# One-core gated spectral and token-MLP kernel: renumbered odd wavenumbers, pairs of 64-row inverse products, filter rows in two slabs, a 16-partition special line

## Chip, cores and metric

The kernel runs on one core of a Trainium2 chip. The metric is the device time of one execution in microseconds (us); several executions are made and the median is compared. The profile is of one execution more.

## What is computed

```python
x = A_x                                            # 1 x 2048 x 512, bf16
g = sigmoid((x * gate_w).sum(-1, keepdims=True))   # one gate value per row
a = irfft2(rfft2(x.float()) * (w_r + 1j * w_i))    # filter: 2048 x 257 complex
h = layernorm(x)                                   # over d
u = gelu(einsum("bsd,sf->bdf", h, w1) + b1)        # f = 1792
y = einsum("bdf,fs->bds", u, w2) + b2
out = g * a + (1 - g) * y.transpose(0, 2, 1)
```

s (2048 rows) is the direction of the token MLP and of the complex transform; d (512 columns) is that of the real transform. All data are bf16, sums of products f32.

## The kernel before

**Staging.** Row s = 512 q + 4 a + r is kept on partition a. The MLP has two large products, each 14 pieces ft of 128 hidden units by 16 row blocks j, each a full-array 128x512 product: m1 (L716) with W1 (`wa`, `wb`), and m2 (L1065) with W2, whose pieces come into the buffers that W1 has left. The gelu (L732, ScalarE) turns m1's sums into `gl`, the operand of m2; L1071 (ScalarE) or L1078 (VectorE) takes m2's sums out of PSUM.

The spectral branch lies among these products. Forward transform along s: products with the table `ta` (L565 to L568), eviction to `xp`, radix-4 additions on VectorE (L596 to L612); the wavenumbers are split in even ones (lt=0, two halves of 64 partitions) and odd ones (lt=1). Special columns of d are corrected by small VectorE operations (`sp0`, `sp1`, L621 to L639). Forward transform along d (L664), evicted by L671 into `X`; `tb2` (L680 to L688) makes sums and differences of mirrored rows into `B`. The filter: `W` holds w_r and w_i in the order of the wavenumbers, `wt` rows that have to be mirrored over the partitions by a product with a flipped identity (`flip`, L768, evicted by L772); `wprep` (L789, L790), and the complex multiplication on VectorE (`bfly` L831/832, `mul` L839, `comb` L844/845, `ob` L851 to L853). Column 0 and 256 have their own small path (`c0a` L800/801, `c0b` L820 to L825, `c0c` L858/859), and wavenumber 1024 (the "special line") is worked on one partition (`nyq`, L810 to L815), goes with eight lines more by DMA into `s9`, through one product (`linem`, L871, evicted L873), and back into `B` by a DMA. `omg` (L752 to L754) makes (1-g)/2-like factors out of the gate.

Inverse along s: radix-4 on VectorE, then products with the table `ti`: even residues (L929 to L934), odd residues of the odd wavenumbers as full-array 128x256 products (`i1`, L925), odd residues of the even wavenumbers as 64-row products in two halves of the array (`i1s`, L897). ScalarE evicts them (L900, L940, L945), VectorE joins the halves (`eo2` L905, `zf` L953 to L959, `fq` L965/966). Inverse along d: `i3` (L1008 to L1012), evicted with the gate as factor by L1016, joined by L1025 and L1042 to L1049, added to the MLP part (L1078, L1084) and stored.

**What sets the order.** Every step is a task with an engine, an author's duration, the tasks it depends on, a priority and PSUM banks that it takes and frees (`add`, L151). `order` (L173) runs through time by these durations, lets each engine take the ready task of lowest priority number, and so writes one list; the instructions are emitted in this order and each engine runs its own in order. Banks: "acc" four, "fa" two, "fb" two. A matmul task for m1 or m2 is one product, an inverse task one group of products.

**Loads.** All loads are issued by SyncE (SP) through `dma` (L312) in one queue; each waits in the built program for one of eight semaphores in turn, that is for the load eight before it. Order: x and tables, W1's first columns (`wa`, `wb`), `b2h` (8-byte packets), the filter `ld_W(0)` of w_r, W1's last columns (`wb`), `ld_W(1)` of w_i, then W2 into `wa` and `wb`, with the inverse tables `ti` (in the buffer "rot") and `tg` between. `ld_W` makes 16 DMAs for a component, among them four "turned" ones, in which the rows are read in descending order within slabs:

```python
for e in range(4):
    dma(W[:, 1, e, 1, 0:257], v[:, 3 - e, 3, :].rearrange("(o i) l -> o i l", o=4)[:, ::-1])
for o in range(4):
    dma(W[32 * o:32 * o + 32, 1, :, 0, 0:257], v[96 - 32 * o:128 - 32 * o, :, 1, :])
```

Of the kernel before, what the change touches and what calls it, by code (L numbers as in the profile page):

```python
# [16 lines left out]
P = 128  # L17
# [13 lines left out]
def ti_at(r):  # L31
    return (0, 1024, 512, 1920)[r], (512, 896)[r % 2]


def make_tables():

    p = np.arange(P)
    r4 = np.arange(4)
# [6 lines left out]
    ti = np.zeros((P, 3072))  # L45
    for r in range(4):
# [6 lines left out]
        th = ang(s, 1 + 4 * (p ^ 96), S)  # L53
# [7 lines left out]
        if r % 2:  # L61
            sg = np.where(p < 64, 1.0, -1.0)[:, None]
            th = ang(k, s, S)
            v = v.reshape(P, 7, P)
            v[:, 0] = np.cos(th)
            v[:, 1] = sg * np.cos(th)
            v[:, 2] = -np.sin(th)
            v[:, 3] = -sg * np.sin(th)
            v[0, 2:4] = alt * (0.5 ** 0.5 if r == 1 else -(0.5 ** 0.5))
            th = ang(1 + 4 * (p ^ 96), s, S)  # L70
            v[:, 4] = -np.sin(th)
            v[:, 5] = np.cos(th)
            v[:, 6] = np.sin(th)
            ti[:, o:o + w] = v.reshape(P, w)
        else:
            s5 = np.append(s, 512)
            for lt, kk in enumerate((k, 1 + 4 * (p ^ 96))):
                th = ang(kk, s5, S)
                c, n = np.cos(th), -np.sin(th)
                if lt == 0:  # L80
                    n[0, 0:P] = 0.0 if r == 0 else -alt
                u = v[:, 256 * lt:256 * lt + 256]
                u[:, 0:P], u[:, P:] = c[:, 0:P], n[:, 0:P]
                if r == 0 and lt:
                    u[:, P] = -n[:, P]
                elif r == 0:
                    ti[:, 2816:2879], ti[:, 2943:3007] = n[:, 2:P:2], n[:, 1:P:2]
                    u[:, 0:65], u[:, 66:130] = c[:, 0:129:2], c[:, 1:P:2]
                    u[0, 66:130], ti[0, 2879:2943] = 0.0, 1.0
# [49 lines left out]
class Plan:  # L139
# [33 lines left out]
    def order(self):  # L173
# [17 lines left out]
        while events:  # L191
# [19 lines left out]
            while progress:  # L211
                progress = False
                for eng, ts in pending.items():
# [57 lines left out]
def kernel(  # L271
# [42 lines left out]
    def alloc_first():  # L314
# [15 lines left out]
        t["wn"] = sb([1, 2, WL], BF16, "wn")  # L330
# [3 lines left out]
        t["sp"] = sb([P, 4, 2, 4], F32, "sp")  # L334
# [3 lines left out]
        t["cm"] = sb([P, 4, 4, 2], F32, "cm")  # L338
# [95 lines left out]

    def ld_W(comp):
# [24 lines left out]
    def ld_ti():  # L460
        t["ti"] = sb([P, 3072], BF16, "rot")
# [158 lines left out]
    def sp0():  # L620
        V.tensor_copy(t["sp"][:], t["X"][:, 0, :, :, :, 0])  # L621
    dk = [("D", r) for r in range(4)]
    add("DVE", tiny(1), sp0, reads=dk, writes=["sp"], prio=0)

    def sp1():
        sp, sd, fx = t["sp"], t["sd"], t["fx"]
# [7 lines left out]
        V.tensor_scalar_mul(sd[:, 0, 0, 1], sd[:, 1, 1, 1], c)  # L634
        V.tensor_scalar_mul(sd[:, 1, 0, 1], sd[:, 0, 1, 1], -c)
        V.tensor_add(fx[:, 1, 0], sp[:, 0, 1], sd[:, 0, 0, 1])
        V.tensor_sub(fx[:, 3, 0], sp[:, 0, 1], sd[:, 0, 0, 1])
        V.tensor_sub(fx[:, 1, 1], sd[:, 1, 0, 1], sp[:, 2, 1])
        V.tensor_add(fx[:, 3, 1], sd[:, 1, 0, 1], sp[:, 2, 1])  # L639
    add("DVE", tiny(12), sp1, reads=["sp"], writes=["fx"], prio=0)  # L640

    for lt in (0, 1):
# [3 lines left out]
               dk + ([] if lt else ["sp"]), [("Z", lt, 0), ("Z", lt, 1)], pr, False)  # L646
# [9 lines left out]
    for lt in (0, 1):  # L656
        for e in (0, 2, 1, 3):
# [16 lines left out]

            if e >= 2:
                def tb2(lt=lt, e0=e - 2):
# [13 lines left out]
                add("DVE", tt(1024) + 2 * tt(508) + tiny(6) * (e > 2), tb2, reads=[("R", lt, i, c) for i in (e - 2, e) for c in range(2)],  # L690
                    writes=[("B", lt, i) for i in es_], prio=2.5)


# [57 lines left out]
    def omg():  # L751
        V.tensor_scalar(t["omg"][:], t["g"][:], -0.5, 0.5, op0=Alu.mult, op1=Alu.add)  # L752
        V.tensor_scalar(t["g"][:], t["g"][:], 0.5, 0.5, op0=Alu.mult, op1=Alu.add)
        V.tensor_mul(t["ombb2"][:], t["omg"][:], t["b2h"][:].rearrange("p q r -> p (q r)"))  # L754
    add("DVE", 0.4, omg, reads=["b2h"], writes=["g", "omg"], prio=0)


    add("SP", 0.2, ld_ti, writes=["ti"], prio=39, nbytes=754176, after=[pl.last_w["pa", r, dq] for r in range(4) for dq in range(4)])
# [35 lines left out]
    for lt in range(2):  # L794
# [3 lines left out]
        def c0a(lt=lt):  # L798
            b, c0 = t["B"][:, lt], t["c0"][:, lt]
            V.tensor_copy(c0[:, :, 0, :], b[:, :, 0:2, 0])  # L800
            V.tensor_copy(c0[:, :, 1, :], b[:, :, 3:1:-1, 0])
        add("DVE", 0.2, c0a, reads=bk, writes=[("c0", lt)], prio=0)
        if lt == 0:
            def nyq():
                pz = sb([1, 1280], F32, "X")
                na = pz[:, 0:1024].rearrange("p (i v l) -> p i v l", i=2, v=2)
                nn = t["nn"] = pz[:, 1024:1280].bitcast(BF16).rearrange("p (v l) -> p v l", v=2)
                wn, v = t["wn"], t["B"][0:1, 0, 0, 2:4, :]
                for i in range(2):
                    V.tensor_mul(na[:, i], v, wn[:, i, None, 0:L].to_broadcast([1, 2, L]))  # L810
                V.tensor_sub(nn[:, 0], na[:, 0, 1], na[:, 1, 0])
                V.tensor_add(nn[:, 1], na[:, 1, 1], na[:, 0, 0])
                V.tensor_mul(pz[:, 0:2], t["c0"][0:1, 0, 0, 1, :], wn[:, 0, 0:257:256])
                V.tensor_add(nn[:, 0, 0:1], pz[:, 0:1], pz[:, 1:2])
                V.tensor_sub(nn[:, 1, 0:1], pz[:, 0:1], pz[:, 1:2])  # L815
            add("DVE", 3 * d1(512) + 0.35, nyq, reads=[("B", i, e) for i in range(2) for e in range(4)] + [("W", 0), ("W", 1), ("c0", 0)] + pbk, writes=["nn"], prio=0.5)

        def c0b(lt=lt):
            c0, cm, ce, pm = t["c0"][:, lt], t["cm"], t["ce"][:, lt], t["wpm"]
            V.tensor_mul(cm[:, 0], c0[:, :, 0], pm[:, 0, lt])  # L820
            V.tensor_mul(cm[:, 1], c0[:, :, 1], pm[:, 1, lt])
            V.tensor_mul(cm[:, 2], c0[:, :, 0], pm[:, 1, lt])
            V.tensor_mul(cm[:, 3], c0[:, :, 1], pm[:, 0, lt])
            V.tensor_sub(ce[:, :, 0], cm[:, 0], cm[:, 1])
            V.tensor_add(ce[:, :, 1], cm[:, 2], cm[:, 3])  # L825
        add("DVE", tiny(6), c0b, reads=[("c0", lt), "wpm"], writes=[("ce", lt)], prio=0.3)
# [35 lines left out]
        if lt == 0:  # L862
            def lines():
                t["s8"] = sb([P, D], BF16, "s8")
                dma(t["s9"][0:8], t["B"][0:1, 0].rearrange("p e (c v) l -> p (e c) (v l)", c=2))
                dma(t["s9"][8:9], t["nn"].rearrange("p v l -> p (v l)"))
# [19 lines left out]
    i1t = {}  # L886
    for rs, h in ((0, 0), (0, 1), (1, 0), (1, 1)):
        if rs:
            def i1s(h=h):
                p2 = t["i1s", h] = [ps([P, 2, 2, P], F32, tag, 2) for tag in ("fa", "fb")]  # L890
                for n, r in enumerate((1, 3)):
                    ti = t["ti"][:, ti_at(r)[0]:]
                    for v in range(2):
                        for c in range(2):
                            for m in range(2):
                                k = slice(64 * m, 64 * m + 64)
                                T.matmul(p2[m][:, n, v], lhsT=t["B"][k, 0, r, 2 * c + v, h:L:2], rhs=ti[k, 2 * c * P:2 * c * P + P], start=(c == 0), stop=(c == 1))  # L897
            i1t[h, 1, 0] = i1t[h, 3, 0] = add("PE", MMR, i1s, reads=[("T", 0, 1), "ti"], writes=[("i1s", h)], prio=3, alloc=["fa", "fb"])
            for m in range(2):
                add("ACT", act(512), lambda h=h, m=m: A.copy(t["zo"][:, h, m], t["i1s", h][m][:]), reads=[("i1s", h)] + pbk, writes=[("zo", h, m)],  # L900
                    prio=1.7, free=[("fa", "fb")[m]], after=[lined])

            def eo2(h=h):
                for k, f in enumerate((V.tensor_add, V.tensor_sub)):
                    f(t["zz"][:, 1, h, 0, :, k].rearrange("p v r a -> p r v a"), t["zo"][:, h, 0], t["zo"][:, h, 1])  # L905
            add("DVE", 2 * tt(512), eo2, reads=[("zo", h, m) for m in range(2)], writes=[("zz", h, r, 0) for r in (1, 3)], prio=3.55)
        for r in (rs, rs + 2):
            for lt in range(rs, 2):
                tag = ("fa", "fb")[lt if not rs else r // 2]

                def i1(h=h, r=r, lt=lt, tag=tag):
                    if "zz" not in t:
# [220 lines left out]
```

## Time and profile before

| | |
|---|---|
| median of 3 executions | 126.05 us (125.95 to 126.53) |
| profiled execution | 126.11 us, span 124.3 us, granted TensorE clock 1.000 |
| TensorE (PE) busy | 119.8 us, 96%, 789 products |
| VectorE (DVE) busy | 113.2 us, 91%, 271 instructions |
| ScalarE (ACT) busy | 83.7 us, 67%, 176 instructions |
| DMA | 23.10 MB, mean 186 GB/s |
| m1 (L716), all groups | 27.0 + 17.1 + 9.9 + 6.1 us busy |
| m2 (L1065), two large groups | 24.7 + 24.0 us busy |

The span is the time from the first to the last instruction; the execution's own time is 1.8 us longer. PE's busy time is that of pipelined products; what a product costs in a row of others is read from the distance of the starts (0.216 us for 128x512), not from its duration of 372 to 379 ns. The page's DMA line (busy tenths in 40 slices of 3.1 us) and the rate under it show when the loads run:

```profile
DMA  3999999992459946699999930000000000003751
GB/s 112 316 329 306 397 394 385 376 300 62 112 121 258 289 97 121 157 395 406 420 414 415 422 132 0 0 5 0 3 0 0 5 0 0 0 12 131 287 211 42
```

### The profile page before, as it was taken

The numbers are of one execution on the slowest core, as the hardware profiler recorded it, in microseconds if no ns is written. First come the engines' busy times: TensorE is split into PE (matmuls) and PEld (weight loads), VectorE is DVE, ScalarE is ACT, GpSimd is POOL, SyncE is SP. The second block draws the span as 40 slices with busy tenths as digits, with TensorE's granted clock in tenths as the row PEclk, the third lists the DMA queues.
The fourth block names the chain that finished last, engine by engine and source line by source line (L and its number), as shares of the span: only waits on it lengthen the run. The fifth ranks groups of instructions, "written<-read, shape, count | busy, mean of one in ns | idle before, by whom it ended". The sixth has DMA issues, their size and how long they took to land.

```text
span 124.3 us, 2226 instructions
## 1 busy us (share of the span) xinstructions
PE 119.8 (96%) x789; PEld 67.7 (54%) x789; DVE 113.2 (91%) x271; ACT 83.7 (67%) x176; POOL 0.2 (0%) x4
## 2 busy tenths in 40 slices
PE   7799999999999999999999999999999999999990
PEld 2245555555645466644445555555577576665590
DVE  1789999999999999999999999999969999999951
ACT  3696889699999999999520003742279999993200
POOL 0000000000000000000000000000000000000000
PEclk9999999999999999999999999999999999999999
DMA  3999999992459946699999930000000000003751
GB/s 112 316 329 306 397 394 385 376 300 62 112 121 258 289 97 121 157 395 406 420 414 415 422 132 0 0 5 0 3 0 0 5 0 0 0 12 131 287 211 42
DMA packets 18203, 23.10 MB, mean 186 GB/s; under 512 B 2174, under 2 KB 15888, under 8 KB 18192
## 3 DMA queue, kind: packets, MB, share of 16 engines
q1 hardware_dynamic: 17616, 22.34, 52.9%
q10 hardware_dynamic: 576, 0.62, 1.6%
q8 instruction: 6, 0.10, 0.3%
q14 instruction: 5, 0.04, 0.1%
HBM read 20.84 MB, written 2.10 MB: 185 GB/s over the span
## 4 chain that ended last, share of the span: by engine, by line
PE 93%; DMA 2%; DVE 1%; ACT 0%; issue 0%
PE acc L1065 33%; PE acc L716 31%; PE fb L716 6%; PE fb L1065 6%; PE fa L716 3%; DMA x<-in_A_x_dram 2%; PE fb L664 1%; PE fa L664 1%; PE fa L565 1%; PE fa L566 1%; PE fa L897 1%; PE fb L1012 1%; PE fa L1012 1%; PE fa L568 1%; PE fa L567 1%; PE fb L925 1%
## 5 line engine op out<-in xcount | busy, mean ns | idle before, releaser
L716 PE MATMUL acc<-h,wb 128*128 128x512 bf16 x112 | 27.0, 379 | 0.0
L1065 PE MATMUL acc<-gl,wb 128*128 128x512 bf16 (+1 forms) x98 | 24.7, 372 | 0.0
L1065 PE MATMUL acc<-gl,wa 128*128 128x512 bf16 (+1 forms) x98 | 24.0, 371 | 0.0
L1071 ACT ACTIVATE x<-acc,ombb,omg 128x512 bf16<-128x512 f32 x12 | 9.0, 780 | 19.3 <-PE acc L1065 19.3
L1065 PEld LDWEIGHTS <-wa 128*128 128x128 bf16 x126 | 13.4, 113 | 9.6
L1065 PEld LDWEIGHTS <-wb 128*128 128x128 bf16 x126 | 13.2, 114 | 9.4
L716 PE MATMUL acc<-h,wa 128*128 128x512 bf16 x64 | 17.1, 379 | 0.0
L716 PEld LDWEIGHTS <-wb 128*128 128x128 bf16 x112 | 10.7, 98 | 10.3
L716 PEld LDWEIGHTS <-wa 128*128 128x128 bf16 x112 | 10.3, 98 | 10.9 <-DMA wa<-in_B_w_dram 1.1
L489 DVE BATCH_NORM_STATS2 stats<-x 128x6 f32<-128x512 bf16 x12 | 8.1, 676 | 2.1 <-DMA x<-in_A_x_dram 2.1
L746 ACT ACTIVATE x<-x 128x512 bf16<-128x512 bf16 x16 | 10.0, 654 | 0.0
L571 ACT CAST xp<-fa 128x512 bf16<-128x512 f32 x16 | 9.0, 594 | 1.5 <-PE fa L568 1.4
L716 PE MATMUL fb<-h,wa 128*128 128x512 bf16 x32 | 9.9, 379 | 0.0
L732 ACT ACTIVATE gl<-acc,b1f 128x512 bf16<-128x512 f32 x11 | 7.8, 711 | 2.8 <-PE acc L716 2.8
L537 ACT ACTIVATE h<-x,nmr,rstd 128x512 bf16<-128x512 bf16 x11 | 8.4, 806 | 1.3 <-DVE nmr L528 1.1
L716 PE MATMUL fa<-h,wa 128*128 128x512 bf16 x16 | 6.1, 378 | 0.9 <-DVE h L531 0.9
L664 PEld LDWEIGHTS <-X 128*128 128x128 bf16 x64 | 4.7, 98 | 2.2
L1016 ACT ACTIVATE B<-fb,g 128x512 bf16<-128x512 f32 x8 | 5.5, 689 | 0.0
L1016 ACT ACTIVATE B<-fa,g 128x512 bf16<-128x512 f32 x8 | 5.5, 685 | 0.0
L671 ACT CAST X<-fb 128x512 bf16<-128x512 f32 x8 | 5.1, 639 | 0.0
L671 ACT CAST X<-fa 128x512 bf16<-128x512 f32 x8 | 5.1, 635 | 0.0
L741 DVE TENSOR_TENSOR x<-x,gw 128x2048 bf16<-128x2048 bf16 x4 | 4.7, 1214 | 0.0
(183 smaller groups left out, 234.8 us busy)
## 6 DMA issues: line engine op xcount, KB each, us to landing
wb<-in_B_w_dram SPq DMA_DIRECT2D x11, 512.0 KB
wa<-in_B_w_dram SPq DMA_DIRECT2D x7, 512.0 KB
wa<-in_B_w_dram SPq DMA_DIRECT2D x2, 896.0 KB
wb<-in_B_w_dram SPq DMA_DIRECT2D x4, 384.0 KB
out_dram<-x SPq DMA_DIRECT2D x3, 512.0 KB
x<-in_A_x_dram SPq DMA_DIRECT2D x2, 512.0 KB
wa<-in_B_w_dram SPq DMA_DIRECT2D x4, 224.0 KB
rot<-dft_ti SPq DMA_DIRECT2D x1, 768.0 KB
```

The source lines that it names most:

```text
L489: V.bn_stats(out=t["stats"][:, j, :], in_=t["x"][:, j // 4, j % 4, :])
L537: add("ACT", 0.71, lambda j=j: A.activation(t["h"][:, j // 4, j % 4, :], t["x"][:, j // 4, j % 4, :], ActF.Identity, bias=t["nmr"][:, j:j ...
L571: add("ACT", act(512), lambda r=r, dq=dq: A.copy(xe(r)[:, :, :, dq, :], t["pa", r, dq][:]), reads=[("pa", r, dq)], writes=[("X", r, dq)], ...
L664: T.matmul(pb[:, k % 2, k // 2], lhsT=t["X"][:, lt, EX[e], c, k, :], rhs=tbl(k, c), start=True, stop=True)
L671: A.copy(t["X"][:, lt, EX[e]].rearrange("p c j l -> p (c j l)").rearrange("p (h c g b) -> p h c g b", h=2, c=2, b=2)[:, :, c], t["pb", lt, ...
L716: T.matmul(t["u", ft][:], lhsT=w[:, j // 4, j % 4, c * P:(c + 1) * P], rhs=t["h"][:, j // 4, j % 4, :], start=(j == jorder[0]), stop=(j == ...
L732: gelus.append(add("ACT", act(512, 1) , lambda ft=ft: A.activation(t["gl"][:, ft, :], t["u", ft][:], ActF.Gelu_apprx_tanh, bias=t["b1f"][: ...
L741: add("DVE", tt(2048), lambda r=r: V.tensor_mul(t["x"][:, :, r, :], t["x"][:, :, r, :], t["gw"][:, None, :].to_broadcast([P, 4, D])), read ...
L746: A.activation(t["x"][:, q, r, :], t["x"][:, q, r, :], ActF.Copy, accum_out=t["glog"][:, 4 * q + r:4 * q + r + 1])
L1016: A.activation(eo_v(p)[:, n].rearrange("p h (n w) -> p h n w", w=2), t["i3", j][:].rearrange("p h (w n) -> p h n w", w=2), ActF.Copy, scal ...
L1065: T.matmul(t["y", j, m][:, cs], lhsT=w[:, o, 512 * q + r:512 * q + 512:4], rhs=t["gl"][:, ft, cs], start=(ft == 0), stop=(ft == NFT - 1))
L1071: A.activation(tbuf(j).rearrange("p h d -> p (h d)"), t["y", j, 0][:], ActF.Identity, bias=t["ombb2"][:, j:j + 1], scale=t["omg"][:, j:j + 1])
```

## The change

- Odd wavenumbers are numbered `sig = 2*(p%64)+1-p//64` on partition p (before `p^96`), so that those of one parity lie in one half of the partitions. The odd residues' products of the odd wavenumbers are then 64-row products too (`i1s` for lt 0 and 1), and `eo2` gets a second form for lt=1, with four VectorE operations. A group for h=1 follows directly on that for h=0 and takes no banks of its own: h=0 takes all four of fa and fb. `order` counts how many banks of a kind a task wants. The table `ti` falls from 3072 to 2112 columns.
- The filter rows follow the new numbering. The turned rows are read in two slabs of 64 rows rather than four of 32; those of w_r go ahead of `wt`, those of w_i are issued at the end of `ld_W(0)`, ahead of W1's last columns. The strided rows of residue 1 come in two DMAs rather than four.
- The special line is spread over 16 partitions: `vs` is fetched out of `B` by two DMAs issued by ScalarE, `nn` goes to `s9` by two.
- Small operations: `sp0` dropped and `sp1` 12 to 10; `tb2`'s edges in three operations for lt=0, one for lt=1, whose two copies ScalarE makes (`tb2c`); `c0a` and the affine part of `omg` on ScalarE, `c0b` 12 to 6 operations; two copies of `zf` in one.

```diff
-        th = ang(s, 1 + 4 * (p ^ 96), S)
+        th = ang(s, 1 + 4 * sig, S)
...
-                        if t.ready <= now + 1e-9 and all(caps[a] > 0 for a in t.alloc):
+                        if t.ready <= now + 1e-9 and all(caps[a] >= t.alloc.count(a) for a in t.alloc):
...
+    def turned(comp):
+        for e in range(4):
+            dma(t["W"][:, comp, 1, e, 1, 0:257], wsrc[comp].rearrange("(e i h k) l -> k e h i l", e=4, h=2, k=4)[3, 3 - e][:, ::-1])
...
             W, u = t["W"][:, comp], t["wt"][:, comp]
+            if comp == 0:
+                turned(0)
             dma(u[64:127, :, 0:257], v[65:128, :, 0, :])
...
-            for e in range(4):
-                dma(W[:, 1, e, 1, 0:257], v[:, 3 - e, 3, :].rearrange("(o i) l -> o i l", o=4)[:, ::-1])
-            for o in range(4):
-                dma(W[32 * o:32 * o + 32, 1, :, 0, 0:257], v[96 - 32 * o:128 - 32 * o, :, 1, :])
+            for n in range(2):
+                dma(W[64 * n:64 * n + 64, 1, :, 0, 0:257], v[1 - n::2, :, 1, :])
...
-            dma(t["wn"][:, comp, 0:257], wsrc[comp][1024:1025, :])
+            dma(t["wn"][:, comp, 0:16], wsrc[comp][1024, 0:256].rearrange("(a b) -> a b", b=16))
+            if comp == 0:
+                dma(t["wn"][0:1, 0, 16:17], A_w_r[1024:1025, 256:257])
+                turned(1)
...
-        add("SP", 12.3, ld_W(comp), writes=[("W", comp), ("wt", comp)], prio=17 + 8 * comp, nbytes=300000, after=[a0])
+        add("SP", (14.6, 7.7)[comp], ld_W(comp), writes=[("W", comp), ("wt", comp)], prio=17 + 8 * comp, nbytes=300000, after=[a0])
...
-                        for i in range(2):
-                            bh, vh = b[:, i::2], v[:, 2 * i:2 * i + 2]
-                            V.tensor_sub(bh[:, :, 1:3, 0], vh[:, :, 0, 0:4:3, 0], vh[:, :, 1, 0:4:3, 0])
-                            V.tensor_copy(bh[:, :, 0:4:3, P], vh[:, :, 0, 1:3, 0])
-                            V.tensor_copy(bh[:, :, 1:3, P], vh[:, :, 1, 1:3, 0])
+                        V.tensor_sub(*tb2e(lt, 1, 0), tb2v(lt)[:, :, :, 1, 0:4:3, 0])
+                        if lt == 0:
+                            for k in (0, 2):
+                                V.tensor_copy(*tb2e(lt, k, P))
...
+    add("ACT", 0.45, tb2c, reads=[("R", 1, i, c) for i in range(4) for c in range(2)], writes=[("B", 1, i) for i in range(4)], prio=4.4)
...
+    def omga():
+        A.activation(t["omg"][:], t["g"][:], ActF.Copy, bias=0.5, scale=-0.5)
+        A.activation(t["g"][:], t["g"][:], ActF.Copy, bias=0.5, scale=0.5)
+        A.activation(t["g"][64:P, 1:NJ:2], t["g"][64:P, 1:NJ:2], ActF.Copy, scale=0.5 ** 0.5)
...
+            def nspread():
+                for v in range(2):
+                    dma(t["vs"][:, v], t["B"][0:1, 0, 0, 2 + v, :].rearrange("p (a b) -> p a b", b=16), A)
...
     for rs, h in ((0, 0), (0, 1), (1, 0), (1, 1)):
-        if rs:
-            def i1s(h=h):
-                p2 = t["i1s", h] = [ps([P, 2, 2, P], F32, tag, 2) for tag in ("fa", "fb")]
+        for lt in range(2 * rs):
+            def i1s(h=h, lt=lt):
+                zalloc()
+                p2 = t["i1s", h, lt] = [ps([P, 2, 2, P], F32, tag, 2) for tag in ("fa", "fb")]
...
+                            f = (320 - 64 * c) if lt else c * P
                             for m in range(2):
                                 k = slice(64 * m, 64 * m + 64)
-                                T.matmul(p2[m][:, n, v], lhsT=t["B"][k, 0, r, 2 * c + v, h:L:2], rhs=ti[k, 2 * c * P:2 * c * P + P], start=(c == 0), stop=(c == 1))
-            i1t[h, 1, 0] = i1t[h, 3, 0] = add("PE", MMR, i1s, reads=[("T", 0, 1), "ti"], writes=[("i1s", h)], prio=3, alloc=["fa", "fb"])
+                                T.matmul(p2[m][:, n, v], lhsT=t["B"][k, lt, r, 2 * c + v, h:L:2], rhs=ti[k, f:f + P], start=(c == 0), stop=(c == 1))
+            i1t[h, 1, lt] = i1t[h, 3, lt] = add("PE", MMR, i1s, reads=[("T", lt, 1), "ti"], writes=[("i1s", h, lt)], prio=-3 if h else 3, alloc=() if h else ["fa", "fb"] * 2, after=[i1t[0, 1, lt]] if h else ())
...
+                zv = t["zz"][:, 1, h, 1].rearrange("p v k r a -> p r (v k) a")
+                x = lambda u: u.rearrange("p r v (k a) -> p r (v k) a", k=2)
+                V.tensor_add(zv[:, :, :, 0:64], x(e), x(o))
+                V.tensor_sub(e, e, o)
+                V.tensor_sub(zv[:, :, 0:4:2, 64:P], x(e)[:, :, 0:4:2], x(e)[:, :, 1:4:2])
+                V.tensor_add(zv[:, :, 1:4:2, 64:P], x(e)[:, :, 0:4:2], x(e)[:, :, 1:4:2])
...
-            for lt in range(rs, 2):
-                tag = ("fa", "fb")[lt if not rs else r // 2]
+            for lt in range(0 if rs else 2):
+                tag = ("fa", "fb")[lt]
...
-                        if r % 2:
-                            for c in range(2):
-                                f = (5 - c) * P
-                                T.matmul(p1[:, v], lhsT=d(c), rhs=ti[:, f:f + L], start=(c == 0), stop=(c == 1))
```

In the built program (the order per engine is known without a time) `wf` of w_r (L768) stands ten m1 products later on PE, the first inverse group 18 m2 products earlier, L871 some 20 earlier, the last `i3` some 23 earlier against the end; the two groups of 32 64-row products have eight m2 products between them.

More of the change, by code (lines that the diff above doesn't have):

```diff
@@ L633, in sp1 @@
         V.tensor_scalar_mul(fx[:, 2, 1], sd[:, 1, 1, 0], -1.0)
[L634 to L640, printed above, removed]
+        for i, k in ((1, c), (3, -c)):
+            V.scalar_tensor_tensor(fx[:, i, 0], sd[:, 1, 1, 1], k, sp[:, 0, 1], op0=Alu.mult, op1=Alu.add)
+        for i, f in ((1, Alu.subtract), (3, Alu.add)):
+            V.scalar_tensor_tensor(fx[:, i, 1], sd[:, 0, 1, 1], -c, sp[:, 2, 1], op0=Alu.mult, op1=f)
+    add("DVE", tiny(10), sp1, reads=dk, writes=["fx"], prio=0)
     for lt in (0, 1):
@@ L796, with c0a @@
         bk = [("B", lt, e) for e in range(4)]
[L798 to L802, printed above, removed]
-        if lt == 0:
-            def nyq():
[L805 to L810, printed above, removed]
+        if lt == 0:
+            def c0a():
+                b, c0 = t["B"], t["c0"]
+                A.copy(c0[:, :, :, 0, :], b[:, :, :, 0:2, 0])
+                A.copy(c0[:, :, :, 1, :], b[:, :, :, 3:1:-1, 0])
+            add("ACT", 0.45, c0a, reads=[("B", i, e) for i in range(2) for e in range(4)], writes=[("c0", i) for i in range(2)], prio=4.5)
@@ new lines @@
+        if lt == 0:
+            def nspread():
+                for v in range(2):
+                    dma(t["vs"][:, v], t["B"][0:1, 0, 0, 2 + v, :].rearrange("p (a b) -> p a b", b=16), A)
+            b0 = [("B", 0, e) for e in range(4)]
+            add("DMA", 3.5, lambda: None, reads=b0, writes=["vs"], after=[add("ACT", 0.12, nspread, reads=b0, prio=2)])
+            def nyq():
+                na, nn, wn, e = t["na"], t["nn"], t["wn"], t["na"][0:1, 0, 0, 0:2]
+                V.tensor_mul(na[:], t["vs"][:, None].to_broadcast([16, 2, 2, 16]), wn[:, :, None, 0:16].to_broadcast([16, 2, 2, 16]))
@@ L818, in c0b @@
[L818 to L826, printed above, removed]
+                V.tensor_mul(e, t["c0"][0:1, 0, 0, 1, :], wn[0:1, 0, 0:17:16])
@@ L828, in bfly @@
+        if lt == 0:
+            add("DVE", tiny(6), c0b, reads=[("c0", 0), ("c0", 1), "wpm"], writes=[("ce", 0), ("ce", 1)], prio=3.22)
         def bfly(lt=lt):
@@ L946 @@
-                add("ACT", act(512), i1ev, reads=[("i1", h, r, lt)] + pbk, writes=[("zz" if r % 2 else "ze", h, r, lt)], prio=1.7, free=[tag], after=[lined])
+                        u = ti[:, 256 * lt:256 * lt + 256]
+                        if r == 0 and lt == 0:
+                            T.matmul(p1[:, v, 65:256], lhsT=d(1), rhs=t["ti"][:, 1920:2111], start=True, stop=False)
+                            T.matmul(p1[:, v, 128:192], lhsT=d(0), rhs=u[:, 66:130], start=False, stop=True)
+                            T.matmul(p1[:, v, 0:65], lhsT=d(0), rhs=u[:, 0:65], start=True, stop=True)
+                        else:
+                            T.matmul(p1[:, v, P:], lhsT=d(1), rhs=u[:, P:], start=True, stop=True)
+                            T.matmul(p1[:, v, 0:P], lhsT=d(0), rhs=u[:, 0:P], start=True, stop=True)
@@ L948 @@
+                add("ACT", act(512), i1ev, reads=[("i1", h, r, lt)] + pbk, writes=[("ze", h, r, lt)], prio=1.7, free=[tag], after=[lined])
             if r % 2 == 0:
@@ L959, in zf @@
                         V.tensor_sub(k1[:, :, :, ::-1], e[:, :, :, 0:P], e[:, :, :, P:L])
-                add("DVE", 2 * tt(512) + (tiny(2) if r == 0 else 0), zf, reads=[("ze", h, r, lt) for lt in range(2)], writes=[("zz", h, r, lt) for lt in range(2)], prio=3.55)
+                add("DVE", 2 * tt(512) + (tiny(1) if r == 0 else 0), zf, reads=[("ze", h, r, lt) for lt in range(2)], writes=[("zz", h, r, lt) for lt in range(2)], prio=3.55)
         def fq(rs=rs, h=h):
```

135 lines of the change are left out of this document (69 added, 66 removed).

## The prediction

> **What bounds the kernel now.** I read the engines and the chain on the page first, then the timeline of PE around the edited products, then the DMA queue of SP. The page's engine line, and its chain:
>
> ```profile
> PE 119.8 (96%) x789; PEld 67.7 (54%) x789; DVE 113.2 (91%) x271; ACT 83.7 (67%) x176; POOL 0.2 (0%) x4
> PE 93%; DMA 2%; DVE 1%; ACT 0%; issue 0%
> ```
>
> PE runs without a gap from 5.3 us to its last matmul at 121.4; fin L1078 and a store take the remaining 2.9 us. So a PE instruction removed is worth its whole time, as long as PE always has its next operand. The edited products in PE's timeline (start, us, line, tiles, count):
>
> ```profile
> 93.73 0.60 PE L925 MATMUL fa<-rot,B 128*128 128x256 bf16 x4
> 94.17 0.22 PE L933 MATMUL fb<-rot,B 128*128 128x128 bf16 x1
> ...
> 96.14 0.59 PE L1065 MATMUL acc<-gl,wb 128*128 128x512 bf16 x2
> 96.66 0.23 PE L897 MATMUL fa<-rot,B 64*128 64x128 bf16 x1
> 96.67 0.23 PE L897 MATMUL fb<-rot,B 64*128 64x128 bf16 x1
> 96.73 0.22 PE L897 MATMUL fa<-rot,B 64*128 64x128 bf16 x1
> 96.73 0.22 PE L897 MATMUL fb<-rot,B 64*128 64x128 bf16 x1
> ...
> 97.22 0.62 PE L1065 MATMUL acc<-gl,wb 128*128 128x512 bf16 x2
> ```
>
> A group's cost is the distance to the next start: 94.17 - 93.73 = 0.44 us for four full-array 128x256 products. Two 64-row products start within 0.01 us of each other, the next pair 0.055 us later: they run side by side.
>
> The queue's issues, in SP's timeline (start and length of a run of issues):
>
> ```profile
> 23.96 0.43 SPq L312 DMA_DIRECT2D b2h<-in_B_b_dram  x1
> 24.44 2.58 SPq L312 DMA_DIRECT2D wt<-in_A_w_r_dram  x4
> 27.93 7.34 SPq L312 DMA_DIRECT2D W<-in_A_w_r_dram  x11
> 35.67 0.24 SPq L312 DMA_DIRECT2D wn<-in_A_w_r_dram  x1
> 35.99 2.61 SPq L312 DMA_DIRECT2D wb<-in_B_w_dram  x4
> 38.65 2.86 SPq L312 DMA_DIRECT2D wt<-in_A_w_i_dram  x4
> 41.56 8.40 SPq L312 DMA_DIRECT2D W<-in_A_w_i_dram  x11
> 50.22 0.24 SPq L312 DMA_DIRECT2D wn<-in_A_w_i_dram  x1
> 50.70 3.33 SPq L312 DMA_DIRECT2D wa<-in_B_w_dram  x7
> ```
>
> SP issues in order, and a DMA waits for the one eight before it to land. So the first load of W2 (wa at 50.70) stands behind all filter loads. Four stretches of the windows view (length, then busy time of PE, PEld, DVE, ACT and POOL, clock, share of the 16 DMA engines, GB/s):
>
> ```profile
> 29.60:30.50 0.90, 0.90 (x6) 0.39 (x4) 0.90 (x1) 0.89 (x4) 0.00 (x0) 1.00 0.29 76
> 33.40:34.40 1.00, 1.00 (x9) 0.62 (x8) 1.00 (x4) 1.00 (x3) 0.00 (x0) 1.00 0.83 189
> 44.80:47.30 2.50, 2.50 (x26) 1.56 (x24) 2.29 (x4) 2.50 (x7) 0.00 (x0) 1.00 0.29 76
> 51.10:65.20 14.10, 14.10 (x76) 6.98 (x74) 13.82 (x49) 10.47 (x27) 0.00 (x0) 1.00 0.97 376
> ```
>
> In the first and the third the four reversed ("turned") loads of w_r and of w_i run: 0.29 x 16 = 4.6 engines are busy. In the last one W2 comes in at the full rate: a W2 piece (0.524 MB at the page's 395 to 422 GB/s) takes 1.26 us, and what starts late stays late.
>
> **The change, part by part.**
>
> 1. *Products of the odd residues (gain on PE).* Removed: four L925 groups, 4 x 0.44 = 1.75 us. An L897 group now costs eight pairs x 0.055 = 0.44, and 0.24 us around it (0.10 entering the half-array form, 0.11 leaving it, 0.03 more at the next product): 0.68 us, two of them 1.36 us. After it two groups of sixteen pairs stand, h=1 directly behind h=0: 2 x (0.89 + 0.24) = 2.26 us. Gain 1.75 + 1.36 - 2.26 = **0.85 us**, all on the path.
>
> 2. *Four banks at once.* A group now needs both fa and both fb banks free, and PE is in order: L1065 products are queued behind it. Its 1.13 us of products leave four banks to evict on ACT, whose evictions stand 0.48 us apart in the trace: 0.5 (the first half's products) + 4 x 0.48 + 0.15 = 2.6 us after a group's start its banks are free. In the new order eight L1065 products (8 x 0.216 = 1.73) stand before the second group, which so wants them at 1.13 + 1.73 = 2.86. Below: 0. Above: an L1071 (0.78 us) among the evictions costs 0.78 - 0.26 = 0.5. I take 0.1, near the free case.
>
> 3. *DVE.* sp0 goes, sp1 falls from 12 to 10 operations, tb2's six edge copies to three or one, c0b from 12 to 6, c0a and two of omg's go to ACT, the special line from 1 partition (0.41 us each for its long ones) to 16. The stretch 56.57 to 61.15 (L686 to L754, 4.58 us) shrinks to some 1.65 us by spacings of 0.07 to 0.09 us for a small operation, and about 0.7 us go elsewhere: -3.6 us. eo2 for the second half adds four operations, +2.15 us. Net -1.4 us, and 0 on the path: PE has W2 products to fill with while DVE works. If that cover were gone it would be up to 1.4 us of gain. The same holds for the loss of the smaller eo2: i1 begins 18 L1065 products earlier in the new order, so it fits ahead.
>
> 4. *ACT.* Nine small operations more, 0.11 to 0.2 us each, about 1.4 us, in a stretch that is full up to 61 us. Behind them stand the gelus L732, whose readers are the first L1065 products at 63.72, and then ACT waits 12.26 us for L1071. I take 0; without the cover at most 1.4 us.
>
> 5. *The special line's two fetches.* vs is fetched by two ACT-issued DMAs, and nn reaches s9 by two DMAs rather than one. L871 moves some 20 matmuls (4.3 us) up. PE's turn for L871 would be at 76.6, the line's data are ready by 61 plus a store's landing of 2 to 3 us: 0; with the cover gone at most 0.3 us.
>
> 6. *Table of the inverse, 768 to 528 KB.* 0.24 MB at 415 GB/s = 0.6 us less ahead of the last three W2 pieces. Not on the path unless W2 is late.
>
> 7. *The filter loads (the term that decides).* Each turned load reads four slabs of 32 rows before, and two slabs of 64 rows after. The rows: loads with four slabs keep 4.6 engines busy (0.29); loads whose outer extent is 32 partitions 13 (0.83); 128-partition ones 15.5 (0.97). Engines in use follow the outer extent, so two slabs should give two engines. From the stretch at 44.8, whose 379 packets I counted in the DMA view, a packet costs 2.5 x 4.6 / 379 = 0.030 us on its engine. Four turned loads are 512 packets: before 128 on each of four engines = 3.8 us, after 256 on each of two = 7.7 us. The Trainium skill, DMA: Bandwidth & Descriptors, "Why a DMA increments its semaphore by 16 and not by 1", states that the count of engines is the largest number up to 16 which divides the slowest dimension of both sides, and that these are the lowest-numbered ones; its 4 agrees with the 4.6, and by it the two slabs give 2, on engines that all other loads use too.
>
>    The order also changes: turned(w_r) goes first, and turned(w_i) goes ahead of wb, W1's last columns. On the two engines I add: they are free of b2h's 8-byte packets at about 27.0 (DMA view); turned(w_r) 256 packets, the other w_r rows 1536/16 = 96 plus some 24 for loads of 63 rows that use fewer engines, turned(w_i) 256: 632 x 0.030 = 19.0 us; gaps 0.5; wb's 1.57 MB at 400 GB/s 4.0 us; landing 0.5: wb is in at 51.0. wt(w_i) follows at about 52.4 (44 packets). The last three issues of SP wait for these (0.24 to 0.65 us each): the first wa goes out at about 53.4 rather than 50.70, **2.7 us late**. Ends: -0.5 us (three fewer issues, no slower engine), +6 us (each packet at 0.035 us).
>
>    Who waits. L768 for w_i has its turn on PE at 51.65, so about 1 us of stall there. W2 pieces: in the trace of before, piece 9 lands at 65.75 and piece 11 at 70.5 (69.9 with item 6); in the new order their first products stand at 66.5 and 70.7. The slack is 0.75 us. A stall at L768 moves those products back as well, so both together cost 2.7 - 0.75 = **1.95 us**, and not more.
>
> Sum: -0.85 + 0.1 + 1.95 = +1.2 us. The profiled execution took 126.11 us, its span 124.3 (1.8 us lie around it); the median, 126.05, stands 0.06 lower. Forecast 127.3 us.
>
> **Rivals.**
>
> *A. The filter loads stay covered.* If the engines in use do not follow the slabs, or the earlier start of the turned loads pays for their length, W2 starts within 0.7 us of 50.70 and PE never waits. For it: SP has three fewer issues to make, and the page's GB/s stand at 62 to 121 between 28 and 37 us, so that the engines have time to spare there. Against: both stretches of four slabs show the same 4.6, so the number does not come by chance. Time: 126.05 - 0.85 + 0.05 = 125.25, faster. It decides as long as the first wa leaves before 51.4. Chance 0.14.
>
> *B. The delay eats the gain.* W2 starts 0.9 to 2.1 us late (engines 0 and 1 have more time between other loads than I add up). PE waits 0.2 to 1.4 us: 125.45 to 126.65, no change. Chance 0.20.
>
> *C. The pairs do not run side by side,* so that the change does not do what it says. Thirty-two 64-row products in turn, 0.055 each, are 1.78 us a group and the gain becomes -0.9 us: with covered loads 127.0, with my delay 129.1. Against it stand the L897 starts above. Its chance of 0.03 is inside the slower ones.
>
> *D. The eviction becomes the limit of the pairs.* An L1071 lies ahead of each group's evictions: 2 x 0.78 - 0.26 = 1.3 us of PE waiting for ACT in place of item 2's 0.1. With covered loads 126.5, no change; with my delay 128.5. For it: four evictions take 1.92 us and the products that fill the banks 1.13. Against: L1071 comes once in 3 us and ACT is idle before most of them. Chance 0.03, inside the slower ones. The Trainium skill, TensorEngine Tiling (Array Packing), PSUM Bottleneck, states that after tiling the copy out of PSUM may become the bottleneck and that ScalarE and VectorE should share it; by that rule this rival would be the likely one, but before's trace shows no L897 product that waits for ACT, and no run here yet shows a double group.
>
> **How the numbers follow.** My forecast's own cases have a chance of 0.60, C and D 0.06: slower 0.66. Half a per cent (0.63 us) is about what a measurement can tell from no change: the borders are 125.42 and 126.68. B is the middle (0.20), A faster (0.14). The range: downwards it takes in B, and ends at A's border, 125.4; upwards a delay of 4.5 us, a packet at some 0.033 us: 126.05 - 0.75 + 3.75 = 129.05, rounded to 129.1. The forecast's own range is 126.7 to 129.1.
>
> **What would show it.** In the profile after: the first wa issue at about 53.4 in SP's timeline; stretches with a DMA share of about 0.13 to 0.15 while the turned loads run alone; PE or PEld idle at L768 released by a wt DMA, and at L1065 released by wa or wb; a DMA share in the chain above 2%; two L897 groups of 32 products each 1.0 to 1.1 us long, and no 128x256 products. Wrong would be: wa issued before 51.4 with PE seamless (A), or L897 products that start one after another (C), or PE idle at L897 released by ACT (D).

## The result and the profile after

The changed kernel takes 134.36 us (median of 6 executions, 133.4 to 135.6), the kernel before 126.09 us beside it: a ratio of 1.063 (95% interval 1.058 to 1.068). The prediction, 127.3 us with a range up to 129.1, had the sign and the place right and the size wrong: 8.3 us were lost, not 1.2. The profiled execution took 134.27 us, its span 132.5. (Ratios and intervals in this part leave out executions far above a kernel's fastest; medians are of all.)

The engine line and the chain of the page after:

```profile
PE 121.8 (92%) x791; PEld 67.5 (51%) x805; DVE 112.3 (85%) x253; ACT 85.2 (64%) x183; POOL 0.2 (0%) x4
DMA 35%; PE 29%; SPq 18%; DVE 9%; ACT 3%; issue 2%; ACTq 1%; DVEq 0%
```

The chain has left PE (93% before) for DMA and SP's queue: the end is set by loads now. SP's timeline after, the same loads as before:

```profile
24.17 6.68 SPq L307 DMA_DIRECT2D W<-in_A_w_r_dram  x4
30.90 4.06 SPq L307 DMA_DIRECT2D wt<-in_A_w_r_dram  x4
35.01 3.78 SPq L307 DMA_DIRECT2D W<-in_A_w_r_dram  x5
38.84 0.77 SPq L307 DMA_DIRECT2D wn<-in_A_w_r_dram  x2
39.65 3.53 SPq L307 DMA_DIRECT2D W<-in_A_w_i_dram  x4
43.22 4.45 SPq L307 DMA_DIRECT2D wb<-in_B_w_dram  x4
47.71 3.24 SPq L307 DMA_DIRECT2D wt<-in_A_w_i_dram  x4
51.00 6.10 SPq L307 DMA_DIRECT2D W<-in_A_w_i_dram  x5
57.80 3.78 SPq L307 DMA_DIRECT2D wa<-in_B_w_dram  x7
```

The first wa leaves at 57.80, not at 50.70 (before) or 53.4 (forecast). The four turned loads of w_r alone hold SP for 6.68 us; their issues, which took about 0.5 us each before, take up to 2.2 us. The windows of the turned loads, of the wait and of what follows (columns as in the prediction):

```profile
40.50:45.50 5.00, 5.00 (x39) 2.95 (x38) 4.93 (x8) 5.00 (x15) 0.00 (x0) 1.00 0.14 38
52.00:58.00 6.00, 0.46 (x6) 0.13 (x3) 4.65 (x9) 1.56 (x4) 0.00 (x0) 0.71 0.63 108
58.00:61.20 3.20, 3.20 (x11) 1.45 (x12) 0.00 (x0) 0.63 (x2) 0.00 (x0) 0.50 0.80 269
```

A share of 0.14 is 2.2 engines: the turned loads do run on two. In the second window PE works 0.46 of 6 us, and in the third it works all the time at a granted clock of 0.50. PE's timeline there:

```profile
52.01 0.38 PE L728 MATMUL acc<-h,wb 128*128 128x512 bf16 x1
57.92 0.61 PE L784 MATMUL fa<-wt,flip 128*128 128x256 bf16 x2 [5.54 <-DMA wt<-in_A_w_i_dram]
58.33 0.63 PE L728 MATMUL acc<-h,wb 128*128 128x512 bf16 x1
58.75 0.64 PE L784 MATMUL fb<-wt,flip 128*128 128x256 bf16 x2
```

L784 (L768 before) waits 5.54 us for wt of w_i, and for three microseconds behind it a product takes twice its time (58.33 to 58.75: 0.42 us for one of 128x512 that costs 0.216). The edited products (L928 is L897 before):

```profile
100.64 0.23 PE L928 MATMUL fa<-rot,B 64*128 64x128 bf16 x1
100.64 0.23 PE L928 MATMUL fb<-rot,B 64*128 64x128 bf16 x1
100.70 0.22 PE L928 MATMUL fa<-rot,B 64*128 64x128 bf16 x1
100.71 0.22 PE L928 MATMUL fb<-rot,B 64*128 64x128 bf16 x1
...
101.88 1.03 PE L1091 MATMUL acc<-gl,wb 128*128 128x512 bf16 x4 [0.17 <-issue]
103.49 0.23 PE L928 MATMUL fa<-rot,B 64*128 64x128 bf16 x1
...
104.49 1.05 PE L1091 MATMUL acc<-gl,wa 128*128 128x512 bf16 x4
```

They run side by side; the second group lasts 1.00 us. The first seems to last 1.24 and to end in a pause marked "issue", but there the record of one product is missing: the page counts 805 weight loads (PEld) and 791 products, and behind the first group stand seven L1091 records where the program has eight products. One product of 0.216 us fills the pause. In e12 below, whose page counts 805 of both, there is none.

The span's 8.2 us, from the distances of PE's starts: +5.70 around L784, +1.65 at the halved clock, +0.77 at L1091 for W2, +0.25 ahead of an L1034 product (114.06 to 114.36 us), +0.7 at the start (the first product 0.06 later, the first m1 products 0.28 to 0.43 apart instead of 0.216), -0.85 for the pairs: 8.2. The causes of the 0.25 and of the 0.7 stay open.

### The profile page after: what moved, and what is told of

It is laid out like the page before. It is cut to its first block, busy times and chain, and to the rows that moved or that the text cites. A ratio compares the mean times of both kernels' runs of the same rounds, so it can differ in the third digit from the quotient of the medians.

```text
span 132.5 us, 2238 instructions
## 1 busy us (share of the span) xinstructions
PE 121.8 (92%) x791; PEld 67.5 (51%) x805; DVE 112.3 (85%) x253; ACT 85.2 (64%) x183; POOL 0.2 (0%) x4
## 4 chain that ended last, share of the span: by engine, by line
DMA 35%; PE 29%; SPq 18%; DVE 9%; ACT 3%; issue 2%; ACTq 1%; DVEq 0%
PE acc L1091 22%; SPq L307 18%; DMA wa<-in_B_w_dram 16%; DMA wb<-in_B_w_dram 7%; DMA wt<-in_A_w_i_dram 6%; DMA wt<-in_A_w_r_dram 5%; PE fb L1091 5%; ACT h L972 2%; DVE xp L992 2%; DVE xp L991 1%; DVE X L938 1%; DVE h L943 1%; ACTq L307 1%; DVE X L942 1%; PE fa L1091 1%
## 5 line engine op out<-in xcount | busy, mean ns | idle before, releaser
L728 PE MATMUL acc<-h,wb 128*128 128x512 bf16 x108 | 27.6, 392 | 0.1
L1091 PE MATMUL acc<-gl,wb 128*128 128x512 bf16 (+1 forms) x93 | 23.6, 371 | 0.8 <-DMA wb<-in_B_w_dram 0.4
L1091 PE MATMUL acc<-gl,wa 128*128 128x512 bf16 (+1 forms) x97 | 23.6, 372 | 0.1
L1091 PEld LDWEIGHTS <-wa 128*128 128x128 bf16 x126 | 13.4, 114 | 10.0
L1091 PEld LDWEIGHTS <-wb 128*128 128x128 bf16 x126 | 12.9, 113 | 10.2 <-DMA wb<-in_B_w_dram 1.9
L784 PE MATMUL fa<-wt,flip 128*128 128x256 bf16 x4 | 1.0, 340 | 5.5 <-DMA wt<-in_A_w_i_dram 5.5
L358 PE MATMUL fa<-const-float32-0.0 128*128 128x512 bf16 x10 | 4.4, 629 | 0.8 <-PEq L1143 0.8
```

The costliest lines, as they stand in the source:

```text
L358: T.matmul(pw[:], lhsT=zero[:, 0:1].to_broadcast([P, P]), rhs=zero[:, 0:1].to_broadcast([P, D]), start=True, stop=True)
L728: T.matmul(t["u", ft][:], lhsT=w[:, j // 4, j % 4, c * P:(c + 1) * P], rhs=t["h"][:, j // 4, j % 4, :], start=(j == jorder[0]), stop=(j == ...
L1091: T.matmul(t["y", j, m][:, cs], lhsT=w[:, o, 512 * q + r:512 * q + 512:4], rhs=t["gl"][:, ft, cs], start=(ft == 0), stop=(ft == NFT - 1))
```

## The experiments

"Theory" is: two slabs mean two DMA engines, and SP's queue stands behind them. The rivals were the new place in the queue, the author's durations (and so the written order), and later the fetches of vs.

**Slabs or place.** Four kernels that ran on one chip. e1: the turned loads of the changed kernel read 64 rows in ascending order, with the 64 rows as the outermost extent, so that they are no longer tied to two engines:

```diff
-        for e in range(4):
-            dma(t["W"][:, comp, 1, e, 1, 0:257], ...[3, 3 - e][:, ::-1])
+        for h in range(2):
+            for e in range(0, 4, 2):
+                dma(t["W"][64 * h:64 * h + 64, comp, 1, e:e + 2, 1, 0:257], ..."(e i h k) l -> k h i e l"...[3, h][:, e:e + 2])
```

> The changed kernel, but the eight turned loads are read in ascending row order, 64 rows by two quarters each (so w's turned rows are not mirrored: this part of the computation is changed); number of loads, place in the queue and order of all engines are those of the changed kernel. Theory (two slabs mean two DMA engines, and the whole queue waits behind them): first W2 load (wa) at 50 to 52 us instead of 57.8, no wait at L784 or L1091, only the PE gain is left: 125.2 us (124.9 to 125.6). Rival (the new place of the turned loads, ahead of wt and of W1's last columns, is what delays): still over 127.

Measured: 128.51 us (127.35 to 129.47), ratio 1.019 (1.013 to 1.024). The four turned loads of w_r hold SP for 3.13 us instead of 6.68, wa leaves at 51.40, nothing waits at the flip product, and 5.9 of the 8.3 us are gone without a change of place: the slabs are the main cause. But 2 us stay where the theory had none: in the profiled execution (127.35 us) PE waits for W2, 1.1 us at the first product of piece 8 (the ninth of m2) and 0.2 a little later.

e2: the kernel before with two slabs (`o=4` to `o=2` in the turned loads' source):

> The kernel before with its turned loads read in two slabs of 64 descending rows instead of four of 32 (the order of rows within w is changed by it, nothing else). Theory: each component's four turned loads take some 6.8 us instead of 3.8 in which SP cannot get ahead, so wa goes out at 55.5 to 57.5 instead of 50.70; wt stands ahead of them in this order, so L768 does not wait; the W2 products do: 129 to 131.5 us, with waits at L1065 released by wa and wb. Rival (place, not slabs): 126.1, no change.

Measured: 130.05 us (128.69 to 130.75), ratio 1.020 (1.014 to 1.026). wa leaves at 54.94; three waits of 0.8 to 1.0 us at L1065. The slabs alone make the kernel before slower; W2 is 4.2 us later and not 5 to 7.

e3 moves w_i's wt ahead of w_i's turned loads and wb; e4 puts the turned loads back where they were before:

> The changed kernel with the four wt loads of w_i ahead of w_i's turned loads and of W1's last columns. Theory (the queue's total is what is late): no wait at L784, but W2 comes as late as in the changed kernel (wa at 57 to 58), so the products of L1091 wait 5 to 6.5 us: 130.5 to 132.5 us, 2 to 3.5 us better than the changed kernel, for PE's clock should not fall to half in many short waits. Rival (the one wait at L784 is the whole loss, W2 has time): 125.2 to 126.

> The changed kernel with the turned loads, still in two slabs, at the place in the queue where the kernel before has them (behind wt of their component, w_i's behind W1's last columns). Theory (slabs): wa at 55.5 to 57.5, waits at L1091: 128.5 to 131.5 us. Rival (place): 125.2 to 125.8.

Measured: e3 133.30 us (1.054, 1.050 to 1.058), e4 133.06 (1.054, 1.047 to 1.061). The place is worth 1 us. In e3 the wait moves to m1 for wb, in e4 to W2, and both lose clock, which I had not expected of short waits. The window of e4 that follows five waits of 0.8 to 1.1 us each, and that of e2 that follows its three:

```profile
70.70:75.60 4.90, 4.86 (x12) 1.74 (x13) 4.87 (x8) 0.00 (x0) 0.00 (x0) 0.51 1.03 408
68.60:72.00 3.40, 3.40 (x9) 1.13 (x8) 3.40 (x7) 0.00 (x0) 0.00 (x0) 0.50 1.04 429
```

**What is left of e1.** e6 is e1 with one author's duration raised, so that the written order takes piece 7 at the 12th product instead of the 8th, as before; e7 is e1 without the two vs fetches; e10 is the changed kernel with e6's duration.

```diff
-        add("SP", (14.6, 7.7)[comp], ld_W(comp), ...
+        add("SP", (14.6, 10.0)[comp], ld_W(comp), ...
```

> e1_ascending16 (turned rows not mirrored, 16 engines) with one author's duration changed, that of w_i's loads on SP from 7.7 to 10.0, so that the written order uses W2's pieces 7 and 8 as late as the kernel before does (12th and 16th product instead of 8th and 9th). Theory: e1's remaining 2 us are the slack that the shorter durations took out of the order; the waits at L1092 go: 125.2 to 125.8. Rival (W2 itself comes later, by the vs fetches and their two semaphores): 127 and over.

> e1_ascending16 (turned rows not mirrored, 16 engines) without the two vs fetches that ScalarE issues (vs is set to zero once, so the special line's values are left out). Theory of the order (e6): W2's pieces come 0.3 to 0.5 us earlier, a wait of 0.5 to 1.5 us stays: 126.8 to 128. Rival (the fetches and their semaphores are what makes W2 late in e1): no wait, 125.2 to 125.8.

> The changed kernel (turned loads in two slabs by SP) with durations 14.6 and 10.0, the order of e9. Theory (the wait at L784 and W2's delay of 7 us come from the loads and the order can hide only 1 us of them): 133 to 134.5 us, wait at L784 of 5 us and over, then some 3 us at a clock of 0.5. Rival (the author's durations, and so the order, are the main loss): under 130.

Measured: e6 126.43 us (1.003, 1.000 to 1.005), e7 127.77 (1.011, 1.007 to 1.014), e10 133.27 (1.054, 1.050 to 1.057). With all engines the order takes e1's loss down to nearly nothing. Without the fetches PE's waits for W2 stay (1.6 us in e7), so these are not their cause. With two slabs the order is worth 1 us, for wt is late whatever the order is (L784 waits 5.2 us). So the changed kernel lost twice, and the shares depend on what is mended first: from 134.36 us, e1 takes off 5.9 by the slabs and e6 2.1 more by the order; e10 takes off 1.1 by the order and e6 6.8 more by the slabs. These are medians of different sessions, in which the kernel before had 126.09 to 126.41 us.

**A mirrored version that is not slow.** e5: the turned loads, still in two slabs, issued by GpSimd in its own queue once b1f is there; e8 and e9 are e5 with durations (15.5, 11.0) and (14.6, 10.0):

```diff
-            dma(t["W"][:, comp, 1, e, 1, 0:257], ...[3, 3 - e][:, ::-1])
+            dma(t["W"][:, comp, 1, e, 1, 0:257], ...[3, 3 - e][:, ::-1], nc.gpsimd)
...
+    def turns():
+        nc.gpsimd.tensor_copy(sb([P, 1], F32, "gz")[:], t["b1f"][:, 0:1])
+        for comp in range(2):
+            turned(comp)
+    add("POOL", 1.0, turns, reads=["b1f"], writes=["turned"])
```

> The changed kernel with its eight turned loads, still in two slabs, issued by GpSimd in a queue of its own, after b1f is there (about 23 us), instead of by SP. Theory (what costs is that SP's queue stands behind the two engines' work, not the two-slab loads as such): SP has eight issues fewer, wa goes out by 46 to 48 us, no wait at L784 or L1091: 125.2 us (124.9 to 125.7), faster than both kernels. Rival (the packets of the turned loads are the load on the engines, whoever issues them): W2 is as late as in the changed kernel: 130 to 134.

> e5_turned_by_gpsimd (all of the change, the turned loads in GpSimd's queue) with the author's durations of the filter loads on SP at 15.5 and 11.0 instead of 14.6 and 7.7, so that the written order takes 19 products of pieces 0 to 6 before the first of piece 7 (the changed kernel: 7). Theory (e5's 2 us are waits for W2 for which the order has no slack; W2 comes at the same times as in e5): no wait at L1094, only the PE gain and the two new 0.25 us pauses that e1, e5 and e6 all show (behind the first group of pairs, and at the first i3) remain: 126.1 - 0.85 + 0.5 + 0.1 = 125.85, 125.4 to 126.1. Rival (GpSimd's packets slow other things too): 126.5 to 128.

> As e8, with durations 14.6 and 10.0 (the order of e6 and of the kernel before: piece 7 at the 12th product). Theory: waits of 0 to 0.5 us remain, 125.8 to 126.5. Rival (packets): 127 to 128.

Measured: e5 127.97 us (1.007, 1.004 to 1.011), e8 126.84 (1.006, 1.004 to 1.009), e9 127.39 (1.005, 1.002 to 1.008). The executions of e5 lie between 126.06 and 130.10, those of e9 between 125.75 and 128.97. By the medians e5 is 6.4 us better than the changed kernel, but wa leaves at 52.30, not at 46 to 48: w_r's other five loads take 8.54 us to issue beside GpSimd's packets, so half of the rival held.

e5 does not show that a queue of its own is what helps, as its theory has it. The DMA view of 30 to 34 us in e5 and of 29 to 33 us in the changed kernel (queue, kind, packets, MB, share of the 16 engines):

```profile
q0 software_dynamic: 511, 0.36, 62.8%
q1 hardware_dynamic: 329, 0.15, 16.2%
```

The first is GpSimd's queue, the second SP's. Issued by GpSimd, the turned loads keep ten engines busy (0.628 x 16), not two. The queue and the number of engines changed together, and no run separates them.

In e8 no product waits for W2 any more. Of the two pauses of 0.25 us in its expectation, one is the missing record, and the other (ahead of a first product of i3) does not occur in e8. It and e9 wait at the first inverse product (L963) for the line's way back into B, 0.45 us in e8's profiled execution and 1.76 around it in e9's.

e12 is e8 with that DMA's duration raised from 0.5 to 1.4, which starts the inverse four products later:

> e8_gpsimd_more_slack with the author's duration of the line's way back into B (the DMA behind L873) at 1.4 instead of 0.5, so that the written order starts the inverse four L1094 products later. Theory (all of e8's loss against the sum of the PE terms is named: a wait of 0.45 us for that DMA, two pauses of 0.25, a start 0.28 later): the wait goes, 126.2 us (125.9 to 126.6), not to be told from the kernel before. Rival (a wait as long comes up behind it): 126.6 to 127.5 as e8.

Measured: 128.47 us (1.014, 1.011 to 1.017). My theory fell: the wait did not go, it grew to 1.05 us, with 0.69 and 0.63 us for VectorE behind it. ScalarE's timeline in e12 shows where it comes from:

```profile
53.02 0.69 ACT L747 ACTIVATE gl<-acc,b1f 128x512 bf16<-128x512 f32 x1
54.71 1.60 ACTq L307 DMA_DIRECT2D vs<-B  x2
56.35 0.63 ACT L761 ACTIVATE x<-x 128x512 bf16<-128x512 bf16 x1 [2.65 <-DVE B L689]
...
58.53 0.20 ACT L799 CAST W<-fa 128x8 bf16<-128x8 f32 x1
```

ScalarE stands still for 2.65 us before and in the two fetches of vs. They wait for semaphores of the eight which SP's loads go round on. By the trace's semaphore records, the w_i loads that had these two before them landed at 54.63 and 55.77, and the fetches are issued at 54.71 and 55.79. The row's "DVE B L689" is only what came last by the profile: L689 starts at 55.97, behind both issues. The eviction behind them, L799, is what wprep on VectorE waits for (2.6 us in e12), and the filter, the radix and the line's way back follow. e13 and e14 are e9 and e8 with the fetches issued by GpSimd:

```diff
-                    dma(t["vs"][:, v], t["B"][0:1, 0, 0, 2 + v, :].rearrange("p (a b) -> p a b", b=16), A)
+                    dma(t["vs"][:, v], t["B"][0:1, 0, 0, 2 + v, :].rearrange("p (a b) -> p a b", b=16), nc.gpsimd)
```

> e9_gpsimd_slack with the two vs fetches issued by GpSimd instead of ScalarE. Theory (in e9 and e12 ScalarE stands idle 2.3 to 2.7 us before the fetches, because they wait for semaphores of SP's filter loads; the eviction of L799 behind them comes late, with it wprep, L862, the radix and the line's way back, for which L963 waits 0.5 to 1.8 us): ScalarE does not stand still, the wait at L963 goes, 125.9 us (125.5 to 126.3). Rival (the inverse starts 18 products earlier than VectorE can deliver, whatever ScalarE does): L963 waits as in e9, 126.6 to 127.6.

> e8_gpsimd_more_slack with the vs fetches issued by GpSimd. Theory: as e13, and no wait for W2: 125.8 us (125.4 to 126.2). Rival: 126.6 to 127.2, as e8.

Measured: e13 126.03 us (0.998, 0.996 to 1.001), e14 125.91 us (125.72 to 126.24; 0.997, 0.995 to 0.999). The theory holds: all of PE's waits in e14 are

```profile
PE fa L731 <- DMA wa<-in_B_w_dram: 1.4, 1, 1.4
PE fa L358 <- PEq L1146: 0.8, 1, 0.8
PE acc L1094 <- issue: 0.2, 1, 0.2
```

and from the first product of m2 to the last one it takes 56.84 us (63.91 to 120.75), the kernel before 57.68 (63.56 to 121.24): 0.84 us less, all of item 1's 0.85 and no pause (the row with "issue" is the missing record again). 0.35 us of it are lost again ahead of m2, where the first m1 product starts 0.49 us later. e14 computes all of the reference and beats both kernels, the one before by 0.3%: little, but clear of the interval.

**The pairs alone.** e11 is e12 with the odd wavenumbers' products as full-array ones, from another part of the table:

> e12 with the odd wavenumbers' products of the odd residues as full-array 128x256 products again, four at a time into one bank, read from another part of the table (so these values are changed); order, banks, evictions and VectorE's part stay as in e12. Theory of the prediction's item 1: four groups of 0.44 us in place of thirty-two pairs at 0.055 less entry and exit of 0.24: 1.75 - 1.12 = 0.63 us slower than e12. Rival (the pairs gain nothing where ScalarE's evictions set the pace): the same as e12 within 0.2 us.

Measured: 128.74 us (1.020, 1.018 to 1.022) beside e12's 128.47. The medians cannot decide, since waits for VectorE and the line take 1.86 us in e11 and 2.37 in e12 (profiled executions). The rows can:

```profile
105.00 0.60 PE L929 MATMUL fa<-rot,B 128*128 128x256 bf16 x4
105.44 0.60 PE L929 MATMUL fb<-rot,B 128*128 128x256 bf16 x4
105.87 0.60 PE L929 MATMUL fa<-rot,B 128*128 128x256 bf16 x4
106.31 0.60 PE L929 MATMUL fb<-rot,B 128*128 128x256 bf16 x4
106.75 1.03 PE L1097 MATMUL acc<-gl,wa 128*128 128x512 bf16 x4
```

1.75 us for what the pairs of e12 do in 0.99 and 0.13 around it: 0.63 us, as item 1 had it.

## Why the prediction was right and wrong

*Item 1, the pairs:* right. Two groups cost 1.02 (with the missing product put in) and 1.00 us and 0.10 + 0.03 each around them: 2.28, against 2.26. Rival C is out.

*Item 2, four banks:* no L928 product waits for ScalarE in any run; 0 rather than 0.1, and rival D is out. The Trainium skill, TensorEngine Tiling (Array Packing), PSUM Bottleneck, names the copy out of PSUM as what may become the limit; the trace does not show it here, with eight L1091 products between the groups.

*Item 3, VectorE:* right in size. In e6 the sums behind the filter (L865) start at 62.29, before (L844) at 65.66: 3.4 us earlier, for 3.6. VectorE's whole busy time fell by 0.9 us (113.2 to 112.3), for 1.4. As forecast, PE gets nothing of it.

*Items 4 and 5, ScalarE and the fetches:* ScalarE's work grew by 1.5 us (83.7 to 85.2), for 1.4. That the fetches cost nothing was wrong, hidden in the changed kernel by the wait at L784 and bare in e9 and e12. I priced the two fetches by their data (0 to 0.3 us) and did not ask what the issuing engine waits for: 2.65 us of ScalarE (e12), up to 1.8 us of PE (e9).

*Item 7, the filter loads:* the mechanism is right, the term mis-sized: wa went out 7.1 us late, not 2.7, and rivals A and B are out. Two engines (0.14), and 5.0 x 2.2 / 344 packets (DMA view of 40.5 to 45.5) = 0.032 us for a packet, forecast 0.030, hold while the turned loads run alone. What failed is that I let all loads stand ready in the queue, one behind the other on the two engines, with every packet at 0.030: "632 x 0.030 = 19.0 us; gaps 0.5; wb's 1.57 MB at 400 GB/s 4.0 us". SP did not issue them ahead; its issues took up to 2.2 us while the two engines were at work. By the sum, turned(w_i) starts at 38.3 and ends at 46.0; in the trace its packets run from 40.6 to 48.0, and between 39.0 and 40.6 the engines have little to do (share 0.29). wb's last packet is in at 54.1, not 51.0. wt, issued from 47.71 on, is in at 57.9, not 52.4: from 52 to 54 us, where packets of wb, wt and W share the engines, one cost 0.91 x 16 x 2.0 / 555 = 0.053 us (DMA view), not 0.030. So 2 us were lost ahead of wb, 1 us in it and 2.4 behind it, and the 7.1 us lie beyond the upper end that I gave (+6).

By the Trainium skill, DMA: Bandwidth & Descriptors, "Why a DMA increments its semaphore by 16 and not by 1", two slabs give two engines; 0.14 agrees. Its count of engines says nothing of the queue behind them, and that was the larger part (4.4 of the 7.1 us).

*"Both together cost 1.95 us, and not more":* wrong twice. The waits, 5.70 at L784 and 0.77 for W2, come near to 7.1 - 0.75, but a clock of 0.50 came behind them and cost 1.65 us (2.45 in e4). And the slack was not there: I read it for first products at 66.5 and 70.7. In e1 the turn of piece 8 came at 65.73 and PE waited 1.1 us, though wa had left only 0.70 us later than before. So it is partly chance that the waits of the changed kernel fit. e6 shows 2 us hanging on where the written order puts pieces 7 and 8.

*The range:* its upper end took a packet at 0.033 us for the worst. Nothing in it stood for a second-order loss (clock), for SP being held or for a dearer packet on busy engines.

## What to carry to other kernels

A load's shape sets how many DMA engines it uses when SP issues it (share 0.29 with four slabs, 0.14 with two), and one that uses two holds up the loads behind it in the same queue: look at the DMA share of each stretch, and give such loads a long outermost extent (e6), or issue them from GpSimd, where they ran on ten engines here (e5, e14). Count a DMA's semaphore as a wait of the engine that issues it: a small fetch issued by a busy engine can stand behind another engine's loads. Where an order is written from assumed durations, a duration that is too short takes the slack out of everything behind it.

## What was not expected of the hardware

- After a wait of 5.7 us in one piece, or five of 0.8 to 1.1 us within 6 us (e4), or three of together 2.8 us within 3.5 us (e2), the granted clock stood at 0.50 for 3 to 5 us (1.65 us lost in the changed kernel, 2.45 in e4). After two waits of together 2.0 us (e7) and after 1.3 us (e1) it stayed at 1.00. Where the border lies between these was not measured.
- An issue of SP took up to 2.2 us instead of 0.52 while the turned loads ran on two engines.
- The same two-slab loads ran on two engines when SP issued them (share 0.14) and on ten when GpSimd did (62.8% of 16).
- A pause marked "issue" can be a missing record: 14 products are missing from the changed kernel's trace (791 records, 805 weight loads). The pause behind the first group of 64-row pairs is one of them.
- The cause of the later start of the first m1 product (5.33 to 5.84 us, before 5.29) stays open.
